# First half batch of a fused attention and MLP kernel: its leaky ReLUs on VectorE alone, its output copies in five buffers

## The chip, the cores and the metric

The kernel runs on one core of a Trainium2 chip. Its time is the device time of one execution in microseconds (us), given as the median of several runs. The engines of the core are TensorE (PE in the profile; its weight loads are PEld), VectorE (DVE), ScalarE (ACT), GpSimd (POOL) and SyncE (SP); SP and POOL here mostly issue DMAs. All of them run in parallel, each through its own list of instructions in order, and wait for each other through semaphores.

## The reference

Three stages, cut to what matters. The attention is a landmark one with a pseudo-inverse; its result feeds two MLPs.

```python
def reference(**kwargs):
    attn_out = _attn_ref(**attn_kwargs)               # 4 batches, 8 heads, 576 tokens, 64 wide
    x = attn_out.transpose(0, 2, 1, 3).reshape(B * S, H * D)
    x = _moe_ref(x=x, **moe_kwargs)                   # 2304 x 512, 2048 hidden
    return _moe2_ref(x=x, **moe2_kwargs)

def _moe_ref(x, w_in, w_out, alpha):
    h = x @ w_in
    g = np.maximum(h, 0.0) + alpha * np.minimum(h, 0.0)   # the leaky ReLU
    return (g @ w_out).astype(np.float32)

def _moe2_ref(x, w_in, w_out):
    h = x @ w_in
    g = h * np.clip(h + 3.0, 0.0, 6.0) / 6.0
    return (g @ w_out).astype(np.float32)
```

The weights come in 64-bit words. The kernel narrows them itself: of each tile of 128x512, ScalarE treats the high and the low words (lines 196 and 199, a pair of instructions) and VectorE joins them (line 206).

## The kernel before, in words

The first MLP is done in eight half batches of 288 tokens, `Block1(b, blk)`, each with 16 hidden tiles (items `at_` = 0 to 15, called item 0, item 1 and so on here). `first` computes a hidden tile `h` (128x288) with six matmuls into one of two PSUM buffers and applies the leaky ReLU; `second` multiplies it by a row of `w_out` into four accumulators (`acc`). The second MLP is done in five `Block2` of 512 or 384 tokens with 16 items each; at its end `second` copies each accumulator (`oacc`) into an output tile `ob` and sends that to memory.

In the first half batch (`plain`, b = blk = 0) the products with `w_out` are single fp32 matmuls (line 783); later they are three passes over split operands. Its leaky ReLU has two forms. Items with an even number use VectorE alone: line 757, t = min(h, 0) * (alpha - 1), then line 760, gs = t + h. Items with an odd number use ScalarE and VectorE: line 764, t = relu(-h), then line 765, gs = beta * t + h. The second instruction of each releases the PSUM buffer of `h`, which the item two later writes.

What runs beside the first half batch: the narrowing of the 16 tiles of `w_out` (`wo_gen`; the tiles are called `words`) and of the last quarters of `w_in` (`w_gen`), which the loop emits a few items ahead of their use; `project`, once in four items, which multiplies a quarter of `w_in` by an attention factor (line 677) and splits the result into a high part (ScalarE, line 128, `w<-wp`) and a rest (VectorE, line 129) for the next four items; and parts of the attention of this batch and the next.

TensorE and SyncE run in the order written in the program. `second` follows `first` two items later, for item 0 three. So TensorE's order at the start is: h of items 0, 1, 2; project for items 4 to 7; h of item 3; the products of items 0 and 1; h of item 4; the product of item 2; h of item 5; and so on. ScalarE and VectorE run in an order that a planner makes at build time: by the order of emission among what it thinks ready. An edge can be added to that. The narrowing for item `at_` is queued behind the leaky ReLUs two and three items before it, each instruction only behind those on its own engine:

```python
                        with behind(started if at_ < 3 else steps[at_ - 2] + steps[at_ - 3]):
                            gen.step(max(0, upto - emitted[i]))
```

`steps` and `self.last` hold the instructions of each leaky ReLU: of an odd item one on ScalarE and one on VectorE, of an even item of the first half batch one on VectorE.

The pool `mm` holds `t` (2 buffers), `gs` (5 buffers, 128 x 2 x 288) and `ys` (2 buffers), which the first MLP uses for its results and the second for `ob`.

Of the kernel before, what the change touches and what calls it, by code (L numbers as in the profile page):

```python
# [10 lines left out]
F32 = mybir.dt.float32  # L11
# [5 lines left out]
ALU = mybir.AluOpType  # L17
# [47 lines left out]
def kernel(  # L65
# [26 lines left out]
    NT, DM = out.shape  # L92
    FF = alpha.shape[0]
    P = 128
# [28 lines left out]
    def pool(name, bufs=1, st=ctx, **kw):  # L123
        return st.enter_context(tc.tile_pool(name=name, bufs=bufs, reuse_waits="tile", **kw))

    def split(hi, lo, src, rest=nc.vector):
        return (
            nc.scalar.copy(hi, src),  # L128
            rest.tensor_tensor(out=lo, in0=src, in1=hi.bitcast(F32), op=ALU.subtract),  # L129
        )  # L130

    def passes(ps, lhs, rhs, first=True, last=True):
        for i, (x, y) in enumerate(PASSES):
            nc.tensor.matmul(ps, lhsT=lhs(x), rhs=rhs(y), start=first and i == 0, stop=last and i == 2)  # L134
# [6 lines left out]
    beta = const.tile([P, NK], F32, name="beta")  # L141
# [20 lines left out]
    mm = pool("mm", 2)  # L162
# [455 lines left out]
    def part(b, at_):  # L618

        return (at_ + b % 2 * (NC // 2)) % NC  # L620
# [88 lines left out]
    with tc.manual_schedule(engines=set(first)):  # L709
        ps_idle = two("idle")  # L710

        def warm(n):
            for _ in range(n):
                nc.tensor.matmul(  # L714
                    ps_idle.rearrange("p (a c) -> p a c", a=4), lhsT=idle, rhs=idle.unsqueeze(1).broadcast_to([P, 4, P]),
                    start=True, stop=True,
                )

        warm(8)
        att0 = attention(0, lambda nm: banks[-1](nm), 0, early, rest, warm)  # L720
        next(att0)
        nc.sync.dma_start(out=alpha_sb, in_=alpha.rearrange("(k p) -> p k", p=P))
        for i, _ in enumerate(att0):
            if i == 2 * NTI:
                nc.vector.tensor_scalar(out=beta, in0=alpha_sb, scalar1=-1.0, scalar2=1.0, op0=ALU.mult, op1=ALU.add)
                nc.vector.tensor_scalar(out=minus, in0=alpha_sb, scalar1=1.0, scalar2=None, op0=ALU.subtract)
        project(0, 0, slice(0, 256))
        next(early)
        started = project(0, 0, slice(256, 512))
        for _ in range(2):  # L730
            next(early)
# [8 lines left out]
    class Block1:  # L740
# [5 lines left out]
        def first(self, at_):  # L746
            h = ps_h.tile([P, 512], F32, tag="h", name="h")[:, :HS]
            wt, cs = wts[self.b, at_ // 4], slice(at_ % 4 * P, (at_ % 4 + 1) * P)
            kk = 4 * part(self.b, at_ // 4) + at_ % 4
            at, ts = a_t[self.b], slice(self.blk * HS, (self.blk + 1) * HS)  # L750
            for g in range(NG):
                passes(h, lambda i: wt[g][:, i, cs], lambda i: at[:, i, g, ts], g == 0, g == NG - 1)
            plain = self.b == self.blk == 0
            t = mm.tile([P, HS], F32, tag="t", name="t")
            gs = mm.tile([P, 2, HS], F32 if plain else F32R, tag="gs", name="gs", bufs=5)
            if plain and at_ % 2 == 0:
                nc.vector.tensor_scalar(
                    out=t, in0=h, scalar1=0.0, scalar2=minus[:, kk:kk + 1], op0=ALU.min, op1=ALU.mult
                )
                self.last = [nc.vector.tensor_tensor(out=gs[:, 0], in0=t, in1=h, op=ALU.add)]  # L760
                steps.append(self.last)
                return gs
            self.last = [
                nc.scalar.activation(out=t, in_=h, func=AF.Relu, scale=-1.0),  # L764
                nc.vector.scalar_tensor_tensor(  # L765
                    out=gs[:, 0] if plain else t, in0=t, scalar=beta[:, kk:kk + 1], in1=h, op0=ALU.mult, op1=ALU.add
                ),
            ]
            steps.append(self.last)
            if not plain:  # L770
                split(gs[:, 0], gs[:, 1], t)
            return gs

        def second(self, at_, gs):
            kk = 4 * part(self.b, at_ // 4) + at_ % 4
            if at_ == 0:
                self.acc = [ps_o.tile([P, 512], F32, tag="o", name=f"acc{m}") for m in range(KM)]
            for m in range(KM):
                if m == 2:
                    yield True  # L780
                acc, ms = self.acc[m][:, :HS], slice(m * P, (m + 1) * P)
                if self.b == self.blk == 0:
                    nc.tensor.matmul(acc, lhsT=words[kk][:, ms], rhs=gs[:, 0], start=at_ == 0, stop=at_ == NK - 1)  # L783
                else:
                    passes(acc, lambda i: wout[kk][:, i, ms], lambda i: gs[:, i], at_ == 0, at_ == NK - 1)
            if at_ == NK - 1:
                t0 = self.b * S + self.blk * HS
                for m in range(KM):
                    if m < 2:
                        ys = mm.tile([P, 2, HS], F32R, tag="ys", name="ys")  # L790
                    else:

                        ys = a_t[self.b][:, :, m - 2, self.blk * HS:(self.blk + 1) * HS]
                    split(ys[:, 0], ys[:, 1], self.acc[m][:, :HS])
                    nc.gpsimd.dma_start(out=y_d[:, :, m, t0:t0 + HS], in_=ys.bitcast(F32))

    class Block2:
# [24 lines left out]
        def second(self, kk, gs):  # L822
            nu = self.n // P
            if kk == 0:
                self.acc = [ps_o.tile([P, 512], F32, tag="o", name="oacc") for _ in range(nu)]
            for m in range(nu):
                passes(
                    self.acc[m], lambda z: gs[:, z, m * P:(m + 1) * P], lambda z: w2[1, kk][:, z],
                    kk == 0, kk == NK - 1,
                )  # L830
                if m % 2:
                    yield True
                if kk == NK - 1:
                    r0 = self.r0 + m * P
                    ob = mm.tile([P, DM], F32, tag="ys", name="ob")
                    if m % 2:
                        nc.vector.tensor_scalar(out=ob, in0=self.acc[m], scalar1=1.0 / 6.0, scalar2=None, op0=ALU.mult)
                    else:
                        nc.scalar.activation(out=ob, in_=self.acc[m], func=AF.Copy, scale=1.0 / 6.0)
                    nc.sync.dma_start(out=out[r0:r0 + P, :], in_=ob)  # L840
# [55 lines left out]
    with tc.manual_schedule(engines={mybir.EngineType.PE, mybir.EngineType.SP}):  # L896
# [6 lines left out]
        for n, (x, kk) in enumerate(items):  # L903
            b, at_ = divmod(n, per) if n < n1 else (B, n - n1)
# [61 lines left out]
            while pend and n >= pend[0][0] + (LOOK + 1 if pend[0][2] == 0 else LOOK):  # L966
                _, x0, kk0, gs = pend.pop(0)
# [3 lines left out]
        while pend:  # L971
            _, x0, kk0, gs = pend.pop(0)
# [31 lines left out]
```

## Time and profile before

| what | us |
|---|---|
| median of 3 runs | 851.62 |
| lowest, highest | 851.11, 853.69 |
| the profiled execution | 852.87 |
| its span, first to last instruction | 851.0 |

The profile is of that one execution; 1.87 us lie outside its span. The mean granted TensorE clock over the span is 0.995 of full speed. In a row of a timeline the numbers are the start and the length in us (of several instructions of a kind, their whole stretch), and the bracket at its end gives how long the engine had been idle and what ended that. In the rows for windows the length of the window comes first, then PE, PEld, DVE, ACT and POOL, each with its busy us and its count of instructions, then the granted clock (1.00 is full), the DMA share and GB/s. The chain that ended last runs 95% of the span through TensorE.

### The profile page before, as it was taken

To read this page: it belongs to the slowest core of one execution; us is meant where nothing else is said; L and a number is where in the kernel's file an instruction comes from. 1 tells how busy PE (TensorE), PEld (TensorE's weight loads), DVE (VectorE), ACT (ScalarE), POOL (GpSimd) and SP (SyncE) were. 2 spreads that over 40 slices of the span, in tenths; PEclk is the share of its full clock that TensorE was granted. 3 is DMA by queue.
4 is the path that set the end of the run, shared out by engine and by line. 5 is a ranking of instruction groups with operands and counts; after the bars stand their busy time and mean duration, and the time that the engine had idled before them with its cause. 6 is when DMAs were issued, how large, how long until landed. Compare 5 with 4: busy or idle time off the path is not lost.

```text
span 851.0 us, 13478 instructions
## 1 busy us (share of the span) xinstructions
PE 830.8 (98%) x5437; PEld 720.0 (85%) x5437; DVE 416.9 (49%) x878; ACT 376.9 (44%) x813; POOL 27.6 (3%) x51
## 2 busy tenths in 40 slices
PE   9779999999999999999999999999999999999997
PEld 6457789898998989989998888888888888999896
DVE  5767687556746566456777542322232223222221
ACT  4686465454435435357887632222231223223222
POOL 0000010010101001010101000000000000000000
PEclk9989999999999999999999999999999999999999
DMA  8996312530407201178493000300030003000001
GB/s 254 408 407 171 83 57 57 156 112 2 106 8 197 71 1 57 50 246 330 144 357 130 1 1 7 141 1 0 1 125 1 0 1 124 1 1 37 1 1 38
DMA packets 60847, 82.68 MB, mean 97 GB/s; under 512 B 35696, under 2 KB 43888, under 8 KB 59504
## 3 DMA queue, kind: packets, MB, share of 16 engines
q1 hardware_dynamic: 57648, 68.18, 24.8%
q0 software_dynamic: 3136, 13.63, 4.5%
q8 instruction: 43, 0.70, 0.4%
q14 instruction: 20, 0.16, 0.1%
HBM read 63.45 MB, written 18.35 MB: 96 GB/s over the span
## 4 chain that ended last, share of the span: by engine, by line
PE 95%; ACT 2%; DVE 2%; issue 0%; DMA 0%; ACTq 0%; DVEq 0%
PE h L134 35%; PE oacc L134 23%; PE acc L134 21%; PE acc L783 4%; PE wp L677 2%; PE sa L428 2%; PE tp L271 2%; PE sc L342 1%; PE tp L295 1%; PE psr L512 1%; PE pu L487 1%; PE idle L714 1%; PE atp L458 1%; ACT raw L196 0%; ACT raw L199 0%; PE ctp L471 0%
## 5 line engine op out<-in xcount | busy, mean ns | idle before, releaser
L134 PE MATMUL h<-ysb,w 128*128 128x512 f32 (+1 forms) x960 | 210.1, 368 | 0.0
L134 PE MATMUL oacc<-w,g 128*128 128x512 f32 x864 | 208.9, 390 | 0.0
L134 PE MATMUL acc<-gs,wout 128*128 128x288 f32 x1344 | 206.7, 299 | 0.0
L134 PEld LDWEIGHTS h<-ysb,w 128*128 128x128 f32 x960 | 176.1, 188 | 24.9
L134 PEld LDWEIGHTS oacc<-w,g 128*128 128x128 f32 x864 | 161.7, 188 | 32.3
L134 PEld LDWEIGHTS acc<-gs,wout 128*128 128x128 f32 x1344 | 185.1, 188 | 3.3 <-issue 1.4
L815 DVE SCALAR_TENSOR_TENSOR t<-t,h 128x512 f32<-128x512 f32 (+1 forms) x80 | 50.8, 635 | 216.4 <-ACT t L814 216.4
L814 ACT ACTIVATE t<-h,three 128x512 f32<-128x512 f32 (+1 forms) x80 | 51.7, 646 | 215.1 <-PE h L134 215.0
L134 PE MATMUL h<-a,w 128*128 128x288 f32 x768 | 129.3, 304 | 6.0 <-DVE gs L765 3.9
L134 PEld LDWEIGHTS h<-a,w 128*128 128x128 f32 x768 | 109.0, 189 | 24.3 <-DVE gs L129 10.7
L764 ACT ACTIVATE t<-h 128x288 f32<-128x288 f32 x120 | 49.3, 411 | 71.6 <-PE h L134 70.6
L765 DVE SCALAR_TENSOR_TENSOR t<-t,beta,h 128x288 f32<-128x288 f32 x112 | 57.1, 510 | 40.7 <-ACT t L764 39.9
L129 DVE TENSOR_TENSOR g<-t,g 128x512 fp32r<-128x512 f32 (+1 forms) x80 | 50.9, 638 | 42.3 <-ACT g L128 42.1
L128 ACT CAST g<-t 128x512 fp32r<-128x512 f32 (+1 forms) x80 | 46.0, 577 | 46.2 <-DVE t L815 46.2
L128 ACT CAST gs<-t 128x288 fp32r<-128x288 f32 x112 | 48.5, 433 | 39.5 <-DVE t L765 39.4
L129 DVE TENSOR_TENSOR gs<-t,gs 128x288 fp32r<-128x288 f32 x112 | 50.7, 452 | 25.4 <-ACT gs L128 25.4
L196 ACT ACTIVATE raw<-raw 128x512 f32<-128x512 f32 (+1 forms) x68 | 44.4, 652 | 0.0
L199 ACT ACTIVATE raw<-raw 128x512 int32<-128x512 uint32 (+1 forms) x68 | 44.0, 646 | 0.0
L783 PE MATMUL acc<-gs,raw 128*128 128x288 f32 x128 | 37.1, 429 | 0.0
L783 PEld LDWEIGHTS acc<-gs,raw 128*128 128x128 f32 x128 | 25.0, 207 | 5.9 <-issue 1.0
L206 DVE SCALAR_TENSOR_TENSOR x<-raw 128x512 int32<-128x512 int32 x32 | 22.1, 692 | 13.6 <-ACT raw L199 13.0
L129 DVE TENSOR_TENSOR w<-wp,w 128x512 fp32r<-128x512 f32 (+1 forms) x34 | 20.8, 654 | 14.4 <-ACT w L128 14.2
(172 smaller groups left out, 558.2 us busy)
## 6 DMA issues: line engine op xcount, KB each, us to landing
raw<-in_moe_w_in_dram SPq DMA_DIRECT2D x32, 512.0 KB, 8.0
raw<-in_moe_w_out_dram SPq DMA_DIRECT2D x32, 512.0 KB, 9.0
win<-w_in SPq DMA_DIRECT2D x6, 1024.0 KB, 4.8
ysb<-y_d SPq DMA_DIRECT2D x6, 1024.0 KB, 14.1
y_d<-ys POOLq DMA_DIRECT2D x16, 288.0 KB, 3.1
y_d<-a POOLq DMA_DIRECT2D x16, 288.0 KB, 3.4
out_dram<-ob SPq DMA_DIRECT2D x18, 256.0 KB, 2.0
rk<-in_k_dram SPq DMA_DIRECT2D x16, 256.0 KB, 5.1
```

What stands on the lines that cost most here:

```text
L128: nc.scalar.copy(hi, src),
L129: rest.tensor_tensor(out=lo, in0=src, in1=hi.bitcast(F32), op=ALU.subtract),
L134: nc.tensor.matmul(ps, lhsT=lhs(x), rhs=rhs(y), start=first and i == 0, stop=last and i == 2)
L196: nc.scalar.activation(out=high.bitcast(F32), in_=high.bitcast(F32), func=AF.Prelu, scale=2.0 ** -112, alpha=-(2.0 ** 32))
L199: nc.scalar.activation(out=low, in_=low.bitcast(U32), func=AF.Copy, scale=0.9374 * 2.0 ** -29)
L206: nc.vector.scalar_tensor_tensor(out=to.bitcast(I32), in0=high, scalar=3, in1=low, op0=ALU.logical_shift_left, op1=ALU.bitwise_or)
L271: nc.tensor.transpose(ps[:, j, :n], raw[:n, t, j * P:(j + 1) * P], ident[:n, :n])
L764: nc.scalar.activation(out=t, in_=h, func=AF.Relu, scale=-1.0),
L765: nc.vector.scalar_tensor_tensor(out=gs[:, 0] if plain else t, in0=t, scalar=beta[:, kk:kk + 1], in1=h, op0=ALU.mult, op1=ALU.add),
L783: nc.tensor.matmul(acc, lhsT=words[kk][:, ms], rhs=gs[:, 0], start=at_ == 0, stop=at_ == NK - 1)
L814: nc.scalar.activation(out=t, in_=h, func=AF.Relu, bias=three, scale=1.0),
L815: nc.vector.scalar_tensor_tensor(out=t, in0=t, scalar=6.0, in1=h, op0=ALU.min, op1=ALU.mult),
```

## The change

All 16 items of the first half batch take the form with two VectorE instructions (lines 757 and 760); the form with ScalarE stays for the other half batches, where the split is now unconditional. `steps` and `self.last` of the odd items then hold one VectorE instruction and none of ScalarE. The output tile `ob` moves from the two buffers of `ys` to the five of `gs`, which the second MLP doesn't use otherwise.

```diff
@@ Block1.first
             plain = self.b == self.blk == 0
             t = mm.tile([P, HS], F32, tag="t", name="t")
             gs = mm.tile([P, 2, HS], F32 if plain else F32R, tag="gs", name="gs", bufs=5)
-            if plain and at_ % 2 == 0:
+            if plain:
                 nc.vector.tensor_scalar(
                     out=t, in0=h, scalar1=0.0, scalar2=minus[:, kk:kk + 1], op0=ALU.min, op1=ALU.mult
                 )
@@
             self.last = [
                 nc.scalar.activation(out=t, in_=h, func=AF.Relu, scale=-1.0),
                 nc.vector.scalar_tensor_tensor(
-                    out=gs[:, 0] if plain else t, in0=t, scalar=beta[:, kk:kk + 1], in1=h, op0=ALU.mult, op1=ALU.add
+                    out=t, in0=t, scalar=beta[:, kk:kk + 1], in1=h, op0=ALU.mult, op1=ALU.add
                 ),
             ]
             steps.append(self.last)
-            if not plain:
-                split(gs[:, 0], gs[:, 1], t)
+            split(gs[:, 0], gs[:, 1], t)
             return gs
@@ Block2.second
-                    ob = mm.tile([P, DM], F32, tag="ys", name="ob")
+                    ob = mm.tile([P, DM], F32, tag="gs", name="ob", bufs=5)
```

## Rows read from the trace of the kernel before

**Rows 1.** The page, part 1: busy us, share of the span, instructions.

```profile
PE 830.8 (98%) x5437; PEld 720.0 (85%) x5437; DVE 416.9 (49%) x878; ACT 376.9 (44%) x813; POOL 27.6 (3%) x51
```

**Rows 2.** Windows: the stall, the rest of the half batch, the later half batches.

```profile
44.70:59.66 14.96, 9.50 (x44) 6.90 (x45) 11.44 (x21) 14.96 (x29) 0.54 (x1) 0.77 1.02 416
59.66:112.00 52.34, 51.43 (x313) 39.16 (x312) 35.68 (x71) 31.23 (x67) 1.64 (x4) 1.00 0.49 133
...
112.00:461.00 349.00, 347.62 (x2907) 321.16 (x2906) 225.56 (x521) 192.27 (x464) 22.44 (x35) 1.00 0.39 124
```

**Rows 3.** Waits of PE: for whom, total us, times, longest.

```profile
PE h L134 <- DVE gs L765: 3.9, 1, 3.9
```

**Rows 4.** Timeline of PE, 46 to 61 us.

```profile
46.23 1.03 PE L134 MATMUL h<-a,w 128*128 128x288 f32 x6 [1.54 <-DVE gs L760]
47.19 1.09 PE L677 MATMUL wp<-win,bd 64*32 64x512 f32 x16
52.21 1.81 PE L134 MATMUL h<-a,w 128*128 128x288 f32 x6 [3.93 <-DVE gs L765]
59.66 1.17 PE L134 MATMUL h<-a,w 128*128 128x288 f32 x6
60.67 1.62 PE L783 MATMUL acc<-gs,raw 128*128 128x288 f32 x6
```

**Rows 5.** Timeline of ACT, 50 to 64 us.

```profile
50.89 0.41 ACT L764 ACTIVATE t<-h 128x288 f32<-128x288 f32 x1
51.18 0.71 ACT L196 ACTIVATE raw<-raw 128x512 f32<-128x512 f32 x1
...
52.29 0.71 ACT L196 ACTIVATE raw<-raw 128x512 f32<-128x512 f32 x1
...
55.69 1.08 ACT L128 CAST w<-wp 128x512 fp32r<-128x512 f32 x2
...
63.60 0.41 ACT L764 ACTIVATE t<-h 128x288 f32<-128x288 f32 x1 [2.05 <-PE h L134]
```

**Rows 6.** Timeline of DVE, 47 to 58 us.

```profile
47.30 0.52 DVE L757 TENSOR_SCALAR t<-h,minus 128x288 f32<-128x288 f32 x1 [0.61 <-PE h L134]
51.04 0.69 DVE L206 SCALAR_TENSOR_TENSOR raw<-raw 128x512 int32<-128x512 int32 x1 [0.41 <-ACT raw L199]
51.65 0.51 DVE L765 SCALAR_TENSOR_TENSOR gs<-t,beta,h 128x288 f32<-128x288 f32 x1
52.08 0.45 DVE L760 TENSOR_TENSOR gs<-t,h 128x288 f32<-128x288 f32 x1
54.71 0.69 DVE L206 SCALAR_TENSOR_TENSOR raw<-raw 128x512 int32<-128x512 int32 x1 [0.35 <-ACT raw L199]
56.31 1.29 DVE L129 TENSOR_TENSOR w<-wp,w 128x512 fp32r<-128x512 f32 x2 [0.91 <-ACT w L128]
```

**Rows 7.** The chain that ended last, pieces with start and us.

```profile
54.02 6.02 PE acc L783 x16
60.84 1.94 PE acc L783 x8
```

**Rows 8.** Windows in and behind the stall, for the granted clock.

```profile
51.30:52.20 0.90, 0.00 (x0) 0.00 (x0) 0.90 (x3) 0.90 (x2) 0.00 (x0) 0.55 1.08 451
56.00:58.00 2.00, 2.00 (x5) 1.42 (x5) 1.69 (x4) 2.00 (x5) 0.00 (x0) 0.50 1.02 410
```

**Rows 9.** Timeline of the end, PE and ACT.

```profile
839.39 6.32 PE L134 MATMUL oacc<-w,g 128*128 128x512 f32 x27
844.39 0.60 ACT L839 ACTIVATE ob<-oacc 128x512 f32<-128x512 f32 x1 [3.03 <-PE oacc L134]
847.14 0.60 ACT L839 ACTIVATE ob<-oacc 128x512 f32<-128x512 f32 x1 [2.15 <-DMA out_dram<-ob]
```

**Rows 10.** Timeline between the first two blocks of the second MLP.

```profile
543.07 5.60 PE L134 MATMUL h<-ysb,w 128*128 128x512 f32 x24
543.99 0.60 ACT L839 ACTIVATE ob<-oacc 128x512 f32<-128x512 f32 x1 [1.32 <-DMA out_dram<-ob]
```

## The prediction

> **What bounds the kernel now.** First the page's busy shares: PE is busy for 830.8 of 851.0 us, VectorE and ScalarE for about half [rows 1]. So work saved on VectorE or ScalarE pays only where PE waits for them or runs slowly because of them. The windows say where. From 112 us on through the later half batches PE is busy for 347.62 of 349.00 us, and in the second part of the first half batch, from 59.66 us, for 51.43 of 52.34. Ahead of that, from 44.70 to 59.66 us, it is busy for only 9.50 of 14.96, its granted clock averages 0.77, and ScalarE has no idle time at all [rows 2]. This is the stage with something to gain, and the first two odd items (1 and 3) lie in it.
>
> The list of PE's waits names one large one there: 3.9 us, once, for line 765, the second half of an odd item's leaky ReLU [rows 3]. The timeline shows which. h of item 3 needs the PSUM buffer that item 1's h had. PE ends the projection at 47.19 + 1.09 = 48.28 us and starts item 3 only at 52.21 [rows 4]. In PE's order item 1's h stands ahead of item 2's, which began at 46.23, so it was there by then; but ScalarE, narrowing weights without a pause, came to item 1's line 764 only at 50.89 [rows 5], and VectorE to its line 765 at 51.65 [rows 6]. [...]
>
> The other place is the end: the last output copy waits 2.15 us for the DMA of the first `ob` and starts at 847.14 [rows 9].
>
> **The change part by part.** *The stall.* At most this goes: 3.93 idle, 1.81 - 1.17 = 0.64 and 6.02 - 2 x 1.94 = 2.14, together 6.71 us. How much of it really goes is set by what is late next. With item 1 on VectorE alone, its two instructions have only its h to wait for. VectorE stood idle for 0.61 us ahead of item 2's line 757 at 47.30 and again for 0.41 at 51.04 [rows 6], so I take item 1 to be done by 48.28. Then PE does item 3's h until 48.28 + 1.17 = 49.45 and the two products until 49.45 + 3.88 = 53.33. Item 4 comes next, and it needs the split weights of its projection. ScalarE casts them at 55.69, behind its queue of narrowing work [rows 5]. From that queue only item 1's line 764 is taken; it filled 51.18 - 50.89 = 0.29 us of it. So the casts start at 55.40, the first is done by about 55.94 (half of 1.08), and VectorE's two rests, done at 56.31 + 1.29 = 57.60 [rows 6], come at 57.31. The sixth matmul of item 4 needs the second rest and ends some 0.3 us behind it, at 57.6, where item 4 ended at 59.66 + 1.17 = 60.83 before [rows 4]. That is 3.2 us earlier. A start 0.29 us earlier can let the planner put another half of a narrowing pair in front of the casts (a pair takes 52.29 - 51.18 = 1.11 us [rows 5]), so between 0 and 0.55 goes back; I take 0.3, about the middle. Gain: 2.9 us.
>
> *Behind the stall.* PE was nearly always busy there [rows 2], so the gain stays if data keeps up. The sixth tile of `w_out` is joined at 54.71 + 0.69 = 55.40 [rows 6], while PE starts the third product at 60.67, in the new order about 57.8 [rows 4]; and ScalarE idled 2.05 us ahead of item 5's line 764 [rows 5]. I take 0 for this, covered by three tiles of lead.
>
> *The extra VectorE work.* An item's form of 0.51 us (line 765) becomes one of 0.52 + 0.45 [rows 6]: 0.46 more, 3.7 us over eight items. VectorE had 52.34 - 35.68 = 16.7 us idle in the longer stretch [rows 2], and between the end of an h and the next use of its buffer PE does a product, an h and a product, 1.94 + 1.17 + 1.94 = 5.05 us. So I put it at 0; without that cover it would be at most the 3.7. ScalarE is freed of 8 x 0.41 = 3.3 us, off the path apart from the 0.29 above.
>
> *The five buffers.* At the end, the last copy can start when PE has ended at 839.39 + 6.32 = 845.71 instead of at 847.14 [rows 9]: up to 1.43, and 1.4 with a small delay at the start. Its own DMA then starts that much earlier. At the four block ends inside, the copies wait too (1.32 us in one), but PE meanwhile works on h until 543.07 + 5.60 = 548.67 and doesn't need the accumulators [rows 10]: 0.
>
> *Sum.* 2.9 + 1.4 = 4.3 us. The profiled execution took 852.87, 1.25 above the median; it would become 848.6, and the median 851.62 - 4.3 = 847.3.
>
> **The rivals.** *The clock falls again.* In the forecast PE still idles, from 53.33 to 55.94, 2.6 us. After 1.54 us of idling item 2's six matmuls took 1.03, so at the full clock; after 3.93 the clock was low [rows 4]. 2.6 lies between. If it falls, the slow stretch costs about what it costs now, 0.64 + 2.14 = 2.78: the gain is 4.3 - 2.8 = 1.5, the time 850.1. Chance 0.15, as the gap is nearer to the short one and item 4's first matmuls end it.
> [...]
>
> *The stall stays.* VectorE's queue may hold item 1's second instruction behind the joins of the narrowed tiles, each of which waits for ScalarE. Item 2 shows it: its line 757 was done at 47.82, its line 760 ran at 52.08, although VectorE idled 0.41 us just ahead of the join at 51.04 [rows 6]. If item 1's line 760 runs where line 765 ran, at 51.65, h of item 3 starts at about 52.1 as before and only the end is gained: 850.2. It decides when line 760 of item 1 ends later than 55.94 - 5.05 = 50.9; up to there PE's wait for the casts hides it. Against it: item 1's h is there before item 2's, and item 2's line 757 stood ahead of those joins. Chance 0.18.
> [...]
>
> *ScalarE runs ahead: slower.* The narrowing for an item is queued behind the leaky ReLUs two and three items earlier, on ScalarE only through line 764 of odd items. With those gone nothing paces ScalarE's narrowing. The planner may then put the pairs for items 5, 6 and 7 in front of the casts for item 4. Each costs 1.11 us, and the longer gap brings the slow clock: with five pairs the gain is 3.2 - 5 x 1.11 - 2.8 + 1.4 = -3.8, the time 855.4. It turns into a loss beyond 0.3% from four pairs (3.2 - 4.4 - 2.8 + 1.4 = -2.6). For it: ScalarE has no idle time there and idles 2.05 us later, before a line 764 that goes [rows 2, 5]. Against it: the casts' projection is there from 48.28 us [rows 4], and they were emitted ahead of those pairs. Chance 0.14.
>
> *All of it goes.* If ScalarE's new order brings the casts forward by the 2.6 us that PE would idle, the whole stall and slow stretch go: 6.7 + 1.4 = 8.1, the time 843.5. Nothing in the change calls for that. Chance 0.08.
>
> **How the numbers follow.** Forecast 847.3, chance 0.45. A measurement can tell 0.3%, 2.55 us, from no change. Forecast and "all of it goes" are faster: 0.53. "The clock falls again" and "the stall stays" are within: 0.33. "ScalarE runs ahead" is slower: 0.14. The range reaches from 843.5 to 852.0: it takes in the forecast with its bounds (2.65 to 3.2 for the stall), the two middle rivals with something for the spread of the runs shown, and the best case; it leaves out the slow one.
>
> **What would show it.** Right: PE's wait for line 765 is gone; item 3's h starts near 48.3; PE's first large wait is for the casts `w` ahead of item 4, about 2.6 us at a granted clock of 1.00; the last copy waits for PE, not for a DMA. Wrong: item 1's line 760 behind the joins; more than four narrowing pairs between the projection of item 4 and its casts; a clock of 0.50 after 56 us; or, later, PE waiting for the casts of items 8 to 11 because ScalarE has run on to the last tiles.

## The result and the profile after

The changed kernel takes 863.22 us (median of 4 runs, 862.54 to 863.94) beside 852.15 us for the kernel before. The ratio is 1.0126, with a 95% interval of 1.0113 to 1.0139: 11 us slower, where 847.3 was forecast and 852.0 was the upper end of the range. The profiled execution took 863.94 us with a span of 862.2 (before 852.87 and 851.0) at a mean granted clock of 0.988.

The wait for line 765 is gone from the list of PE's waits, as the change meant it to be. This is the list of the changed kernel (for whom, total us, times, longest):

```profile
PE psr L512 <- DVE nx L529: 7.8, 2, 6.8
PE h L134 <- ACT w L128: 5.8, 3, 3.3
PE wp L677 <- DVE bd L536: 2.1, 2, 1.7
```

In their place stand waits that are larger than the 3.93 us removed [rows 3, 4], and they come *ahead* of the first item of the MLP, inside the attention. The timeline of PE in the changed kernel shows where:

```profile
38.30 1.17 PE L512 MATMUL psr<-nx 128*128 128x96 f32 x4 [6.78 <-DVE nx L529]
...
48.65 0.67 PE L677 MATMUL wp<-win,bd 64*32 64x256 f32 x16 [1.72 <-DVE bd L536]
52.64 0.85 PE L134 MATMUL h<-a,w 128*128 128x288 f32 x2 [3.33 <-ACT w L128]
...
63.59 4.14 PE L782 MATMUL acc<-gs,raw 128*128 128x288 f32 x16
69.69 0.53 PE L134 MATMUL h<-a,w 128*128 128x288 f32 x2 [1.96 <-ACT w L128]
```

Lines 512 and 677 are the attention's inverse and the first projection; the first h starts at 52.64. In the kernel before, PE was past line 512 by 36 us with waits of about one us, and the first h started at 41.32 (the same timeline of before):

```profile
32.22 0.69 PE L512 MATMUL psr<-nx 128*128 128x96 f32 x4 [0.53 <-DVE nx L529]
34.88 0.69 PE L512 MATMUL psr<-nx 128*128 128x96 f32 x4 [1.11 <-DVE nx L529]
...
41.32 0.53 PE L134 MATMUL h<-a,w 128*128 128x288 f32 x2 [0.51 <-ACT w L128]
```

So 11.32 us are lost before the MLP has begun. Who caused it is read from the other two engines. VectorE's line 529 waited for a copy on ScalarE, and ScalarE for a transfer. First DVE, then ACT, of the changed kernel:

```profile
37.95 0.29 DVE L529 TENSOR_TENSOR nx<-psr,nx 128x128 f32<-128x128 f32 x1 [6.57 <-ACT nx L528]
```

```profile
36.32 0.65 ACT L196 ACTIVATE raw<-raw 128x512 f32<-128x512 f32 x1 [6.08 <-DMA raw<-in_moe_w_out_dram]
36.88 0.64 ACT L199 ACTIVATE raw<-raw 128x512 int32<-128x512 uint32 x1
37.42 0.40 ACT L437 ACTIVATE epc<-epc 128x256 f32<-128x256 f32 x1
37.72 0.19 ACT L528 COPY nx<-psr 128x64 f32<-128x64 f32 x1
...
52.21 0.65 ACT L128 CAST w<-wp 128x256 fp32r<-128x256 f32 x2
...
58.84 0.69 ACT L196 ACTIVATE raw<-raw 128x512 f32<-128x512 f32 x1
...
67.95 0.68 ACT L196 ACTIVATE raw<-raw 128x512 f32<-128x512 f32 x1
...
69.05 1.08 ACT L128 CAST w<-wp 128x512 fp32r<-128x512 f32 x2
```

Line 196 is the first half of a narrowing pair, here of a tile of `w_out`. It stood in ScalarE's order in front of the attention's exponential (line 437) and copy (line 528). Its data had not arrived, so ScalarE did nothing for 6.08 us, and the attention's chain of small steps waited behind it. The same three kinds of instruction in the kernel before: the attention's went first, at 31.25 and 31.63, and the first whole tile was narrowed at 37.33, behind them.

```profile
31.25 0.42 ACT L437 ACTIVATE epc<-epc 128x256 f32<-128x256 f32 x1 [0.82 <-DVE epc L436]
31.63 0.21 ACT L528 COPY nx<-psr 128x64 f32<-128x64 f32 x1
...
37.33 0.67 ACT L196 ACTIVATE raw<-raw 128x512 f32<-128x512 f32 x1
```

From 36.32 us on narrowing runs ahead of everything. Between 30 us and the first h the changed kernel narrows 11 pieces of 128x512, the kernel before 2. They stand in front of the first casts too (52.21, the wait of 3.33). Later nine pairs, from 58.84 to 67.95, stand in a row in front of the casts for item 4 (69.05, the wait of 1.96).

The granted clock falls with the idle time, to 0.75 and 0.50. The windows of the changed kernel (length, then PE, PEld, DVE, ACT and POOL, clock, DMA share, GB/s) stand against 1.00 for the whole first 44.70 us before:

```profile
30.00:38.00 8.00, 1.52 (x8) 0.79 (x8) 1.39 (x5) 1.92 (x6) 0.00 (x0) 0.75 1.03 410
38.00:44.00 6.00, 5.63 (x17) 3.19 (x18) 4.89 (x16) 5.67 (x15) 0.00 (x0) 0.50 1.02 408
...
72.00:74.00 2.00, 2.00 (x6) 1.41 (x5) 1.66 (x3) 1.65 (x4) 0.04 (x1) 0.50 1.32 254
```

The account of the profiled executions, as the lag of PE behind the kernel before: +11.32 at the first h (52.64 - 41.32), +10.03 at item 4's (69.69 - 59.66, after the removed stall gave something back and the wait of 1.96 took some of that), about +12 from item 5 on, after the low clock at 72 to 74 us, and +12.43 at PE's last block (851.82 - 839.39). The end gives 1.25 back, and the span is 11.2 longer. In the later half batches the two kernels run alike: from 112 to 461 us PE is busy for 347.61 us, before 347.62 [rows 2].

### The profile page after: what moved, and what is told of

The parts are those of the page before. It is cut to its first block, busy times and chain, and to the rows that moved or that the text cites. A ratio compares the mean times of both kernels' runs of the same rounds, so it can differ in the third digit from the quotient of the medians.

```text
span 862.2 us, 13460 instructions
## 1 busy us (share of the span) xinstructions
PE 836.6 (97%) x5437; PEld 721.8 (84%) x5437; DVE 419.8 (49%) x886; ACT 374.0 (43%) x805; POOL 27.6 (3%) x51
## 4 chain that ended last, share of the span: by engine, by line
PE 91%; ACT 4%; DMA 2%; DVE 1%; SPq 0%; issue 0%
PE h L134 35%; PE oacc L134 23%; PE acc L134 21%; PE acc L782 3%; PE wp L677 2%; ACT raw L199 2%; ACT raw L196 2%; PE sa L428 2%; PE tp L271 2%; DMA raw<-in_moe_w_out_dram 1%; DMA raw<-in_moe_w_in_dram 1%; PE sc L342 1%; PE psr L512 1%; PE tp L295 1%; PE pu L487 1%; PE idle L714 1%
## 5 line engine op out<-in xcount | busy, mean ns | idle before, releaser
L764 ACT ACTIVATE t<-h 128x288 f32<-128x288 f32 x112 | 46.0, 411 | 64.7 <-PE h L134 63.6
```

## The experiments

**The edges alone.** Is it the leaky ReLU's new form that costs, or only that its instruction on ScalarE no longer stands in `steps`? This kernel is the one before, with its old leaky ReLUs, and takes ScalarE's instruction out of the two lists, `steps` and `self.last`, as the change does:

```diff
+            if plain:
+                self.last = self.last[1:]
             steps.append(self.last)
```

> The kernel before, both forms of the leaky ReLU kept; only the ScalarE instruction of the odd items is taken out of the list behind which the narrowing is queued. Theory P (the loss comes from ScalarE's narrowing running ahead of the attention and of the casts, because its pacing hung on line 764): as slow as the changed kernel or slower, 862 to 867 us, with PE's first item near 52.6 us and a wait of some 6 us in the attention around 31.5 to 38. Rival V (the loss comes from the leaky ReLU's move onto VectorE, its 0.46 us more per item and its place in VectorE's queue): no change, 851 to 853.

Measured: 866.92 us, ratio 1.0162 (1.0144 to 1.0179). The new waits and the old one stand together in PE's timeline, and in ScalarE's (second fence) a narrowing again waits for its tile ahead of the attention's instructions:

```profile
38.09 1.17 PE L512 MATMUL psr<-nx 128*128 128x96 f32 x4 [6.38 <-DVE nx L529]
...
65.86 1.81 PE L134 MATMUL h<-a,w 128*128 128x288 f32 x6 [4.10 <-DVE gs L765]
```

```profile
36.12 0.65 ACT L196 ACTIVATE raw<-raw 128x512 f32<-128x512 f32 x1 [5.67 <-DMA raw<-in_moe_w_out_dram]
```

No instruction of this kernel differs from those of the kernel before. The lost edge alone brings ScalarE's narrowing into the attention, and 14 us with it. That it costs more than the change itself fits too: it keeps the wait for line 765 and the old output buffers.

**The edge put back.** The changed kernel, with a copy of one column on ScalarE in each odd item, which does nothing but stand where line 764 stood:

```diff
+    mark = const.tile([P, 1], F32, name="mark")
...
                 self.last = [nc.vector.tensor_tensor(out=gs[:, 0], in0=t, in1=h, op=ALU.add)]
+                if at_ % 2:
+                    self.last.append(nc.scalar.copy(mark, gs[:, 0, 0:1]))
```

> The changed kernel with the pacing put back in another form: in odd items ScalarE copies one column of gs, and this copy of 128x1 stands in the list where line 764 stood. P: the attention is undisturbed, PE's first item starts near 41.3 us, item 3 near 48.3 instead of 52.21, and with the gain at the end of 1.3 the forecast's time comes out, 846 to 849. V: still slow, 858 to 863.

Measured: 854.43 us, ratio 1.0013 (1.0002 to 1.0025). The loss in the attention is gone: the first h starts at 41.60. But the total lies above the 846 to 849 us expected, and is not what the timeline up to 112 us promised. PE, 0.16 us ahead of the kernel before there, fell behind by 4.4 us between 461 and 720 us, at a granted clock of 1.00 and busy for all of these 259.00 us. The copy's target `mark` was a new tile, which moves others, so the next kernel writes into a tile that is there already.

```diff
-                    self.last.append(nc.scalar.copy(mark, gs[:, 0, 0:1]))
+                    self.last.append(nc.scalar.copy(alpha_sb[:, 0:1], gs[:, 0, 0:1]))
```

> As the run with the copy of one column, but the column goes into a tile that exists already (alpha_sb, not read any more), so that no tile moves in SBUF. There PE began the second MLP 0.25 us earlier than in the kernel before, gained 1.3 at the end, and lost some 4 us within the second MLP at a full granted clock. If the 4 bytes by which the new tile shifted the others cause that loss: it is gone, 850.5 to 851.5 for a kernel before of 852.6. If the copies themselves or the change cause it: 854 to 855.

Measured: 850.98 us, ratio 0.9981 (0.9972 to 0.9990), as expected for the case that the new tile caused the loss, and no drift: PE is 0.83 us ahead from 461 us to the end. This is the change as I had pictured it when I predicted, and its PE timeline can be laid beside the forecast's steps:

```profile
48.67 1.05 PE L134 MATMUL h<-a,w 128*128 128x288 f32 x6
49.56 4.04 PE L784 MATMUL acc<-gs,raw 128*128 128x288 f32 x16
56.65 0.53 PE L134 MATMUL h<-a,w 128*128 128x288 f32 x2 [3.04 <-ACT w L128]
57.51 1.00 PE L134 MATMUL h<-a,w 128*128 128x288 f32 x4 [0.33 <-DVE w L129]
58.34 3.76 PE L784 MATMUL acc<-gs,raw 128*128 128x288 f32 x8
```

Item 3's h starts without a wait, its sixteen products take 4.04 us at a granted clock of 1.00 (from 48 to 53 us), and PE then waits 3.04 us for the casts, which start at 56.00. The clock falls to 0.50 behind that wait (windows of the same kernel), eight products take 3.76 us where 1.94 is usual [rows 7], and a lead of 3.01 at item 4 is 0.91 at item 5.

```profile
56.00:58.00 2.00, 1.02 (x5) 0.73 (x5) 1.84 (x3) 2.00 (x6) 0.00 (x0) 1.00 1.03 416
58.00:60.00 2.00, 2.00 (x8) 1.41 (x7) 1.69 (x5) 2.00 (x5) 0.00 (x0) 0.65 1.05 420
60.00:62.00 2.00, 2.00 (x6) 1.41 (x5) 1.23 (x2) 1.68 (x3) 0.53 (x1) 0.50 1.03 408
```

**The output buffers alone**, in the kernel before, and **the leaky ReLUs alone** (the changed kernel without this line):

```diff
-                    ob = mm.tile([P, DM], F32, tag="ys", name="ob")
+                    ob = mm.tile([P, DM], F32, tag="gs", name="ob", bufs=5)
```

> The kernel before with the output tiles alone moved to the five buffers of gs. The forecast's step for the end: the last copy starts when PE ends, 1.4 us earlier, all else in place: 1.2 to 1.4 us below the kernel before. Rival (the DMAs of the last tiles then hinder each other and land later): 0 to 0.5 below.

> The changed kernel with the output tiles back in the two buffers of ys: the leaky ReLU's part alone. If the two parts add, it costs what the changed kernel costs less the 1.3 us that the output buffers alone gained: 863.2 + 1.3 = 864.5 us, ratio about 1.014, with PE's idle stretch near 38 us still 6 to 7 us long, the first item's h near 52.6 us, and the last output copy waiting for a DMA. If the buffers had a part in the loss (sharing the pool of gs), it would come out below the changed kernel, under 863.

Measured: the buffers alone 850.80 us, ratio 0.9985 (0.9976 to 0.9995); the leaky ReLUs alone 863.78 us, ratio 1.0126 (1.0111 to 1.0140). At the end of the kernel with the buffers alone the last copy waits for PE, where it waited for a DMA before [rows 9]:

```profile
844.40 0.60 ACT L839 ACTIVATE ob<-oacc 128x512 f32<-128x512 f32 x1 [0.76 <-PE oacc L134]
```

From PE's end to the span's end it takes 4.0 us in place of 5.3. So the buffers gain 1.3 us, and the loss belongs to the leaky ReLUs. (Between the changed kernel and the one without the buffers the medians show 0.6 us of it, 863.22 and 863.78, less than their runs scatter.) The restored change (0.9981) and the buffers alone (0.9985) differ by 0.0004, 0.3 us, with intervals that overlap: with the pacing put back, the whole work at the stall gains nothing that these runs can tell.

**Two other ways of pacing.** The first lets the narrowing wait only for the first projection (`started`), the second for the latest projection's casts; both are the changed kernel otherwise.

```diff
-                        with behind(started if at_ < 3 else steps[at_ - 2] + steps[at_ - 3]):
+                        with behind(started if at_ < 3 else list(started) + steps[at_ - 2] + steps[at_ - 3]):
```

> The changed kernel; the narrowing for items 3 to 15 also queued behind the casts of the first projection, as that for items 0 to 2 is, and nothing else on ScalarE. P in its first half (most of the loss arises ahead of the first item): PE's first item near 41.3 us and most of the 11 us gone; the narrowing still runs ahead of the casts of items 4 and 8, one pair and some seven pairs more than before, so 849 to 854. If the loss arose mostly behind the first item: 856 to 862. V: 858 to 863.

Measured: 857.78 us, ratio 1.0057 (1.0037 to 1.0076). The attention ahead of the MLP is safe (first h at 41.46), but ScalarE then runs ahead inside the MLP, in front of the casts for item 4 and of an exponential of the attention that runs beside it:

```profile
57.34 0.53 PE L134 MATMUL h<-a,w 128*128 128x288 f32 x2 [4.03 <-ACT w L128]
...
75.69 1.09 PE L428 MATMUL sa<-bdk,qT 128*64 128x64 f32 x8 [4.22 <-DVE sa__862 L444]
```

This is the rival "ScalarE runs ahead" at the place where I had put it, and it costs 5.4 us at PE's end (844.79 against 839.39). That is more than expected: the time lies above the 849 to 854 us named for the case that most of the loss arises ahead of the first item.

```diff
+        cast = started
...
-                        with behind(started if at_ < 3 else steps[at_ - 2] + steps[at_ - 3]):
+                        with behind(started if at_ < 3 else list(cast) + steps[at_ - 2] + steps[at_ - 3]):
...
-                        project(0, at_ // 4 + 1)
+                        cast = project(0, at_ // 4 + 1)
```

> The changed kernel; the narrowing for an item also queued behind the casts of the projection that the loop emitted last, so that those of items 4, 8 and 12 come ahead of it. P, with the forecast's step that the casts for item 4 are next behind the stall: these start near 53.2 instead of 55.7 us, item 4 at about 54 instead of 59.66, the clock does not fall, and the time is 844 to 847. If the casts are not next in line: as with the copy of one column, 846 to 849. V: 858 to 863.

Measured: 849.63 us, ratio 0.9964 (0.9949 to 0.9979). The casts are nearly in time, and PE waits in pieces of 0.74, 0.19 and 0.54 us; the clock falls all the same:

```profile
53.53 0.53 PE L134 MATMUL h<-a,w 128*128 128x288 f32 x2 [0.74 <-ACT w L128]
54.26 0.66 PE L134 MATMUL h<-a,w 128*128 128x288 f32 x3 [0.19 <-DVE w L129]
55.46 0.40 PE L134 MATMUL h<-a,w 128*128 128x288 f32 x1 [0.54 <-DVE w L129]
```

```profile
52.00:54.00 2.00, 1.26 (x6) 0.60 (x4) 1.10 (x2) 2.00 (x5) 0.00 (x0) 1.00 0.98 410
54.00:56.00 2.00, 1.27 (x7) 0.93 (x7) 2.00 (x5) 2.00 (x4) 0.00 (x0) 1.00 1.03 420
56.00:58.00 2.00, 2.00 (x6) 1.42 (x5) 2.00 (x6) 2.00 (x5) 0.00 (x0) 0.50 1.04 420
```

A lead of 6.13 us at item 4 is 3.56 at item 5 and 1.88 at PE's end. The casts (52.88) and item 4 came about where expected, but the clock was expected to hold, and the time lies above both ranges, 844 to 847 and 846 to 849.

**The casts in front.** If the remaining loss is the late casts and the clock behind them, the casts for items 4 to 7 have to go ahead of the narrowing pairs that are emitted with them. This kernel takes the changed one with the in-place copy, emits the projection ahead of the narrowing and queues the narrowing behind the casts. The same order is also tried in the kernel before, without the moved leaky ReLUs.

```diff
-        pend = []
+        pend, cast = [], ()
...
+                    if at_ % 4 == 3 and at_ // 4 + 1 < NC:
+                        cast = project(0, at_ // 4 + 1)
                     for i, (gen, upto) in enumerate(((wo_gen, min(at_ + 2, NK)), (w_gen, min(at_ + 11, NK + 5)))):
-                        with behind(started if at_ < 3 else steps[at_ - 2] + steps[at_ - 3]):
+                        with behind(started if at_ < 3 else list(cast) + steps[at_ - 2] + steps[at_ - 3]):
...
-                    if at_ % 4 == 3 and at_ // 4 + 1 < NC:
-                        project(0, at_ // 4 + 1)
```

> The changed kernel with the copy of one column as in the run before, and the projection emitted ahead of the narrowing of its item, with the narrowing of this and the next three items queued behind its casts. Theory: what keeps the moved leaky ReLU from paying is the wait for the casts for item 4 and the slow clock behind it; with the casts at about 51.4 instead of 55.7 us PE runs through from 48.3, item 4 starts near 53.4 instead of 59.66 at the full clock, and the time is 844.5 to 846.5 for a kernel before of 852.6. Rival (other waits take their place, as the attention's behind the narrowing): 847 to 850.

> The kernel before with the same order of projection and narrowing, its leaky ReLUs as they were. If the casts are next in line only once item 1's leaky ReLU has left ScalarE: item 3 still waits for line 764 until about 52.2 us at a falling clock, and the time is that of the kernel before within 1 us. If the order of the casts alone is worth the gain: 846 to 849.

Measured: 846.83 us for the first, ratio 0.9941 (0.9928 to 0.9954), faster than both kernels of the change; 858.18 us for the second, ratio 1.0067 (1.0054 to 1.0080). The first lies between its two ranges, 844.5 to 846.5 and 847 to 850; the second was in neither of its own. In the first, PE runs from 46.35 us on without a gap until one of 0.46 at 65.36 (timeline, then the window in which the kernel before and the one behind the casts had 0.50):

```profile
49.22 4.04 PE L784 MATMUL acc<-gs,raw 128*128 128x288 f32 x16
52.88 1.16 PE L134 MATMUL h<-a,w 128*128 128x288 f32 x6
53.88 2.10 PE L784 MATMUL acc<-gs,raw 128*128 128x288 f32 x8
...
75.75 0.31 PE L458 MATMUL atp<-ident,epc 64*128 64x64 f32 x2 [1.89 <-DVE epc L448]
```

```profile
56.00:58.00 2.00, 2.00 (x12) 1.77 (x12) 1.42 (x3) 2.00 (x6) 0.00 (x0) 1.00 1.06 408
...
77.00:79.00 2.00, 2.00 (x7) 1.30 (x6) 0.97 (x2) 0.00 (x0) 0.00 (x0) 0.50 0.91 206
```

Item 4's h starts 6.78 us earlier than before (59.66 - 52.88): all of the 6.71 that the prediction put at the stall. Then more than half goes back from 75.75 on, where PE waits 1.89 us for an exponential that stands behind seven narrowing pairs, and runs at the low clock behind that. 2.87 us are left at PE's end in the profiled execution (839.39 - 836.52), and the output buffers add theirs. In the second kernel item 3 still waits 3.94 us for line 765:

```profile
51.76 1.81 PE L134 MATMUL h<-a,w 128*128 128x288 f32 x6 [3.94 <-DVE gs L765]
```

Later waits of 2.18 and 1.96 us, at 81.39 and 93.72 us, come in addition, for attention work that ScalarE does behind narrowing pairs. Of the kernels run here, the order of the casts paid only with the leaky ReLU moved. The moved leaky ReLU, with the pacing put back, gained nothing clear beside the buffers; with the casts in front too it gained clearly more (0.9941 against 0.9985).

**An unread tile, alone.** The kernel before with a constant tile that nobody reads, of 1, 16 and 24 numbers per partition. Tiles begin at multiples of 32 bytes in this program (the first expectation below says 4): all 699 SBUF addresses of the kernel before as built are such multiples, and `three`, one number per partition, lies at 1856 with the next tile at 1888. So 22 of the 32 weight tiles (`w`) of the second MLP and both of `g` move by 32, 64 and 96 bytes, while `ysb`, allocated from the other end, stays:

```diff
-    three = const.tile([P, 1], F32, name="three")
-    nc.vector.memset(three, 3.0)
+    three = const.tile([P, 1], F32, name="three"); mark = const.tile([P, 1], F32, name="mark")
+    nc.vector.memset(three, 3.0); nc.vector.memset(mark, 0.0)
```

> The kernel before with one more constant tile of one number per partition, set once at the start and read by nobody. It moves the tiles allocated behind it by 4 bytes and changes no engine's order. Theory A (the drift of about 4 us in the second MLP of the run with the new tile comes from where the tiles lie): it shows the same here, PE falling behind by 3.5 to 4.5 us between 460 and 715 us at a granted clock of 1.00, the time 855.5 to 857. Theory B (the drift came from the ScalarE copies or from chance): no drift, within 1 us of the kernel before, 852 to 853.

> The kernel before with an unread constant tile of 16 numbers per partition. In this program tiles begin at multiples of 32 bytes, so the tile of one number moved those behind it by 32 bytes; this one moves them by 64. Theory A (what counts is the place within 64 bytes, which is then as in the kernel before): no drift between 460 and 720 us, mean of the 128x512 matmuls of the second MLP's h 389 ns, 852 to 853 us. Theory B (any shift of these tiles against the others costs): a drift of 4 to 4.5 us and 394 ns, as with 32 bytes, 855 to 856 us.

> The same with 24 numbers per partition, which moves the tiles by 96 bytes. Theory A: the place within 64 bytes is that of the shift by 32, so the drift of 4 to 4.5 us comes back, 394 ns, 855 to 856 us. Theory B: also a drift. If it shows none where 64 shows one, both fall.

Measured: 855.02 us, ratio 1.0037 (1.0025 to 1.0050) for 32 bytes, half a us under the range of theory A; 856.64 us, ratio 1.0050 (1.0038 to 1.0063) for 64; 857.48 us, ratio 1.0055 (1.0041 to 1.0069) for 96, the last two 0.6 and 1.5 us above the ranges. All three drift: from 461 to 720 us PE falls behind by 4.4, 4.5 and 4.7 us, in the run with 32 bytes at a granted clock of 1.00 over that stretch. The group of h in PE's instructions by line and shape (count, busy us, mean ns) for 461 to 720 us, of the kernel before and then of the shifts by 32, 64 and 96 bytes:

```profile
L134 PE MATMUL h<-ysb,w 128*128 128x512 f32 x531 | 127.4, 389 | 0.0
```

```profile
L134 PE MATMUL h<-ysb,w 128*128 128x512 f32 x535 | 131.0, 394 | 0.0
```

```profile
L134 PE MATMUL h<-ysb,w 128*128 128x512 f32 x528 | 129.2, 394 | 0.0
```

```profile
L134 PE MATMUL h<-ysb,w 128*128 128x512 f32 x531 | 130.3, 394 | 0.0
```

The same matmuls are 5 ns longer each; those of `oacc` in that stretch take 392 ns in place of 389 with each shift, and the two together make up the drift. Behind 720 us the three differ: from 461 us to PE's last block the lag grows by 3.4, 4.3 and 4.8 us in all, in the order of the three ratios. So the drift in the run with `mark` came from where the tiles lie, not from ScalarE's copies. That the place within 64 bytes decides is refuted by the shift by 64. What in the layout of the kernel before is favourable stays open.

## Why the prediction was wrong

**The step that failed** is one clause: "ScalarE is freed of 8 x 0.41 = 3.3 us, off the path". Line 764 was costed as work, at its 0.41 us. It was worth more as a place in ScalarE's queue: through `behind` it held every narrowing of items 3 and later. The prediction put this term at 0. The leaky ReLUs alone measured 11 us (ratio 1.0126), and the run with the edges alone shows that the removal of that place costs 14 us with not one instruction changed.

**The rival that came true was too small, and in the wrong place.** "ScalarE runs ahead" had the cause right and a chance of 0.14. It looked for the effect next to the stall, between the projection at 48.28 and the casts at 55.69, and counted at most five pairs: 855.4. That effect exists (nine pairs ahead of the casts at 69.05; alone, in the run behind `started`, 5.4 us). But an instruction without an edge goes as soon as the planner thinks it ready, even ahead of work that was emitted before it. That was inside the attention, ahead of 44.70 us, where my reading began. Why the planner took the tile for ready there no record shows. There the first pair cost not its 1.11 us but the time until its data arrived: 6.08 us, in which ScalarE did nothing else. The trace of before held the warning. Its windows show a DMA share of 1.02 and 416 GB/s in the stage [rows 2], and 1.02 and 409 GB/s from 20 to 40 us too. So the DMA engines had no time to spare, and a pair that is moved ahead is likely to find no data. I used that row for its clock and busy times alone.

**The rest of the steps, with the pacing put back** (in-place copy):
- The stall itself was right. Item 3's h was forecast near 48.3 and starts at 48.67, the first h being 0.46 late in that execution; the products were forecast to end at 53.33 and end at 49.56 + 4.04 = 53.60. "The stall stays" (0.18) fell: line 760 of item 1 ran at 47.50, ahead of the joins of `w_out` tiles that wait for ScalarE (only a join of a `w_in` tile that did not wait stood in front of it):

```profile
47.50 0.44 DVE L760 TENSOR_TENSOR gs<-t,h 128x288 f32<-128x288 f32 x1
```

- The casts were forecast for 55.40 and came at 56.00, 0.46 of that being the late start. The late casts were named rightly as the next limit.
- The clock was wrong. The forecast took 2.6 us of idling as nearer to 1.54, where the clock stayed, than to 3.93, where it fell. It measured 3.04, and it fell. "The clock falls again" was priced at 2.78 back, from the kernel before: there item 3's six matmuls took 0.64 us longer than item 4's [rows 4] and the sixteen products behind them 2.14 longer than twice eight later ones [rows 7], at a granted clock of 0.50 from 56 to 58 us [rows 8]. Here the lead went from 3.01 at item 4 to 0.91 at item 5 and 0.75 at the half batch's end, 2.3 back. The restored change is that rival's case: it named a gain of 1.5 us, nearly all of it from the buffers, and the ratio of 0.9981 is one of 1.6.
- The clock does not fall at the same places in every execution. Behind the same gap of 1.11 us in the attention, the four matmuls of line 512 took 0.69 us in the kernel before (at 34.88, above, at a granted clock of 1.00 from 34.67 to 36.00 us) and 1.15 in the restored change (the row below), whose granted clock was 0.52 in the same window; its first h then came 0.46 us later. The kernel with the casts in front varies too: its profiled execution took 848.65 us at a mean granted clock of 0.995, the other three 846.79 to 846.84 at 0.999. In which stretch these differ their records do not show.

```profile
34.67 1.15 PE L512 MATMUL psr<-nx 128*128 128x96 f32 x4 [1.11 <-DVE nx L529]
```

- "All of it goes" (0.08) described what the casts in front then did at item 4, 6.78 of 6.71 us, but something had to call for it, as the text said; the change did not.
- The extra VectorE work was put at 0. In the later part of the half batch the restored change loses no more than 0.16 us (0.91 at item 5, 0.75 at the end), so that holds.
- The five buffers were put at 1.4 and gained 1.25 to 1.3 in the traces; the ratio of the buffers alone gives 1.3 us with an interval of 0.4 to 2.0.

## What to carry to other kernels

Before an instruction is taken off an engine, look up who is queued behind it: its use as a place in the order can be worth several times its own time (here 14 us against 3.3). When an edge goes, ask how early the freed work *can* go, and read the trace there; here one narrowing whose data were still on their way, at a DMA share of 1.03, held ScalarE and the attention behind it for 6.08 us. And where a shorter stall is followed by another wait, the gain counts only as far as the clock holds through it: here 2.3 of 3.01 us went back behind a wait of 3.04.

## What the hardware showed beside that

The granted clock fell to 0.50 not only behind gaps of 3.93, 3.04 and 1.89 us, but also in the kernel that waits for the casts, where PE had no gap over 0.74 us but was busy for only 1.26 and 1.27 us of the two 2 us ahead of it. After the gap of 1.54 us ahead of item 2 it was 1.00 from 46.20 to 48.30 us, and item 2's six matmuls took 1.03 [rows 4]; behind a gap of 1.11 us it held in one kernel and fell in another. The length of one gap alone does not tell these cases apart.

An unread tile in front of the others made the 128x512 matmuls of h 394 ns long instead of 389, and those of `oacc` 392 instead of 389, with each of three shifts: over 4 us from 461 to 720 us. An edit that adds a tile can so bring a difference that has nothing to do with its purpose, and as large as what is looked for here.
